# Values by tokens with TensorE transposes, decays by scans and shifted weight bits in a gated linear-memory layer with a dense expert

## The chip, the cores and the metric

The kernel runs on one core of a Trainium2 chip. The metric is the device time of one execution in microseconds, as the median of several runs. Engines are named as in the profile: PE is TensorE, PEld its weight loads, DVE is VectorE, ACT is ScalarE, POOL is GpSimd, SP is SyncE, whose queue issues most of the DMAs.

## The reference

Two layers follow each other, all in float32. The first is a recurrence over 768 positions in 4 batches of 8 heads with 40 dimensions. For every chain (batch and head) and position:

```python
m_new = maximum(f + m, i)
f_stab, i_stab = exp(f + m - m_new), exp(i - m_new)
C = f_stab * C + i_stab * outer(v, k)
n = f_stab * n + i_stab * k
y = sigmoid(o) * (C @ q) / maximum(abs(n @ q), 1)
```

The second takes the 3072 tokens with 320 features (8 heads of 40) through a dense layer:

```python
h = x @ w_in                       # 320 -> 2048
g = maximum(h, 0) + log1p(exp(-abs(h)))
out = g @ w_out                    # 2048 -> 320
```

The weights arrive as 64-bit words and are turned into single precision on the chip.

## The kernel before, in words

**Steps and tiles.** A step is one batch and one chunk of 128 positions; there are 24, in the order of `ORDER`. Three steps form a tile of 384 tokens, so there are 8 tiles. For a step the kernel makes the masked product of queries, keys and decays (the scores), multiplies it with the gated values and the carried state, divides by the normaliser, multiplies with the sigmoid of the output gate, and writes the result, split into a high and a low float32r part, to `X` with features on partitions. For each tile `products` (L922) then runs 16 blocks: 8 products `hp` of 384 columns (L978), two softplus on ScalarE and a difference on VectorE, and 9 products `po` of 320 columns (L949), 3 in float32 for the first tile.

**The first three steps** (tile 0, `first_tile` from L715) stand by themselves. `first_gates` scans the gates of 128 positions for 32 chains. `first_decays` (L441) lays out the logarithms by a GpSimd mask, sums them on TensorE (`fb`, L455), takes the exponential on ScalarE (L459) and masks again on GpSimd (L460). `scores_pairs` (L577) and `weigh` (L573) follow, `values` (L614) gives values with tokens on partitions, and `split_x` (L700) turns them with three TensorE transposes (`xp`, L706).

**The 21 later steps** (`later_step`, L806) take chunks in two halves of 64 positions. `decays` reads the decay factors broadcast from DRAM, `decay` scans them on VectorE. `scores` (L590) makes 16 state products (L600) and 16 score products (L606). `values_late` (L633) makes 16 products `yq` (L642) that have the values' dimensions on partitions and tokens on columns. `values_wide` copies them, writes them to DRAM (L664), `read_wide` reads them back in the layout of `X` with the normaliser repeated on 16 partitions each (L671 to L679), and `finish_wide` and `end_wide` normalise, gate and split on VectorE (L681 to L698). The output gate of these steps comes transposed (`oT`).

**Weights.** Each of 16 blocks of 640 columns is made of a scaled high word (ScalarE, L218 or L220), three low bits (ScalarE L225 or L230, or GpSimd L227, by the table `Q`), a second scaling for the blocks made later (L233), and an OR on VectorE (L236); then high and low parts follow.

**What sets the order.** The program is recorded in order (`in_order`, L113), so each engine runs its instructions as they were issued. The tables `F` (opening), `W`, `M`, `N` (steps of tiles 3 and later, of tile 1, of tile 2), `Q`, `CI` and `CO` give each piece a place, counted in TensorE products; `tick` (L906) issues what is due. Before a tile's first block, everything that its `X` needs is issued, due or not (L967).

PSUM has 8 banks: three for `hp`, two for all else (`pa`), three for `po`.

Of the kernel before, what the change touches and what calls it, by code (L numbers as in the profile page):

```python
# [8 lines left out]
F32 = mybir.dt.float32  # L9
# [24 lines left out]
C = L // 2  # L34
PP = 64
EP = 48
# [8 lines left out]
def mlstm_moe_kernel(  # L45
# [4 lines left out]
    vko: bass.AP,  # L50
    gates: bass.AP,
    oT: bass.AP,
# [25 lines left out]
    eye = nc.gpsimd.affine_select(  # L78
# [4 lines left out]
    nc.gpsimd.memset(near, 0.0)  # L83
    for base in (0, -C):
        nc.gpsimd.affine_select(
            near, near, pattern=[[0, H], [-1, C]], compare_op=ALU.not_equal, fill=1.0, base=base, channel_multiplier=1
        )
# [15 lines left out]
    fg0 = cpool.tile([NCHAIN, L], F32, name="fg0")  # L103
# [26 lines left out]
    def first_gates():  # L130

        fg = fg0
        ig = p1.tile([NCHAIN, L], F32, tag="sig", name="ig0")
        m = p1.tile([NCHAIN, L + 1], F32, tag="y1", name="m0")
        nc.sync.dma_start(fg, gates[0, :, 0:L])
        nc.sync.dma_start(ig, gates[1, :, 0:L])
        nc.vector.memset(m[:, 0:1], -1e30)
        yield
        nc.vector.tensor_tensor_scan(m[:, 1:], fg, ig, m[:, 0:1], ALU.add, ALU.max)
        nc.vector.tensor_tensor(fg, fg, m[:, 0:L], op=ALU.add)  # L140
        nc.vector.tensor_tensor(fg, fg, m[:, 1:], op=ALU.subtract)
        nc.vector.tensor_tensor(ig, ig, m[:, 1:], op=ALU.subtract)
        nc.vector.tensor_copy(m_end, m[:, L : L + 1])
        nc.vector.memset(fg[:, 0:1], 0.0)
        nc.scalar.activation(ig, ig, AF.Exp)
        pg = ps_a.tile([128, 2, NCHAIN], F32, tag="pa", name="pg0")
        nc.tensor.transpose(pg[:, 1], fg, ident[:NCHAIN, :NCHAIN])
        nc.tensor.transpose(pg[:, 0], ig, ident[:NCHAIN, :NCHAIN])
        nc.scalar.copy(lT, pg[:, 1])
        nc.scalar.copy(gT[:, 0, :], pg[:, 0])  # L150
        done.add(("gT", 0))
        yield
        nc.scalar.activation(fg, fg, AF.Exp)
        nc.vector.memset(fg[:, 0:1], 0.0)
        done.add("fg0")
        yield


    def later_gates():
# [11 lines left out]
        nc.vector.tensor_tensor(fg, fg, m[:, 0:w], op=ALU.add)  # L171
        nc.vector.tensor_tensor(fg, fg, m[:, 1:], op=ALU.subtract)
        nc.gpsimd.tensor_tensor(ig, ig, m[:, 1:], op=ALU.subtract)
        yield Q["GR1"]
        need("fg0")
        nc.scalar.copy(fs[:, 0:L], fg0)
# [16 lines left out]
        pg = ps_a.tile([128, NC - 1, NCHAIN], F32, tag="pa", name="pg")  # L193
# [16 lines left out]
    def single(raw, n, dst=None, slope=False):  # L210
# [74 lines left out]
    def lows():  # L285

        yield Q["LB"]
        for u in range(NF // 2):
# [4 lines left out]
    W = dict(FB=-80, LOAD=-67, Y=-29, SCAN=4, VI=11, VW=16, IQ=20, SP=24, SPD=12, CN=31, CD=36, CE=37, CF=42, YQ=53,  # L293
             YQD=-32, EV=15, YD=61, YD1=3, RD=96, RY=11, RZ=1, NM=138, FIN=146, XH=19, XL=18)
    M = dict(FB=-23, LOAD=-50, Y=-9, SCAN=3, VI=-10, VW=10, IQ=25, SP=27, SPD=12, CN=33, CD=43, CE=49, CF=50, YQ=54,
             YQD=3, EV=47, YD=69, YD1=-30, RD=79, RY=-95, RZ=26, NM=116, FIN=128, XH=-9, XL=15)
    N = dict(FB=-26, LOAD=-57, Y=-7, SCAN=9, VI=-16, VW=22, IQ=23, SP=28, SPD=8, CN=30, CD=34, CE=39, CF=60, YQ=55,
             YQD=6, EV=17, YD=67, YD1=-32, RD=84, RY=-22, RZ=10, NM=125, FIN=150, XH=-9, XL=14)
    Q = dict(Gi0=68, Go0=50, Gi1=-42, Go1=1, Gi2=-47, Go2=36, Gi3=38, Go3=7, Gi4=6, Go4=18, Gi5=-8, Go5=31, Gi6=-10,
             Go6=7, Gi7=4, Go7=35, B3=40, B4=84, B5=125, B6=260, B7=300, B8=368, B9=446, B10=528, S0=-375, S1=-292,  # L300
             S2=-195, GT=-381, GL=52, LB=214, LS=33, SPD=-12, OF0=1, OF1=19, GR0=25, GR1=82, GR2=29, GR3=-26, GR4=18,
             GR5=38, LG=10, FS0=-51, FS1=25, FSW=-14, CI=-48, CO=-4, CS=34, K0=-23, K1=-29, CF=15, RC=-17, RS=92,
             B2=-20, B11=620, GT2=92, GL2=108, FS2=-31, GR6=-1, Hi0=-20, Ji0=63, Hi1=34, Ji1=78, Hi2=16, Ji2=34,
             Hi3=-12, Ji3=49, Hi4=-8, Ji4=-16, Hi5=36, Ji5=136, Hi6=-16, Ji6=107, Hi7=-67, Ji7=20)
# [778 lines left out]
```

## Time and profile before

| | us |
|---|---|
| runs (three) | 462.61 median, 462.57 to 463.05 |
| profiled execution, first to last instruction | 460.2 |
| TensorE busy | 433.4 (94%) |
| VectorE busy | 303.9 (66%) |
| ScalarE busy | 211.2 (46%) |
| GpSimd busy | 137.2 (30%) |

The span of the profiled execution, 460.2, is 2.4 below the median of the runs, which also hold what lies around the first and the last instruction. Busy time is an average over very different stages: 40 us ahead of the first tile's products, the first tile, in which the weights are still being prepared, and seven tiles in which TensorE never stops. A view that cuts the span into stages therefore comes first. In a timeline row the first number is the start, the second the length of the merged group, and "x32" counts its records. A float32 product leaves two records, a transpose and a float32r product one.

### The profile page before, as it was taken

The page shows a single profiled execution, that of the slowest core. Times are in us where ns is not written, and L with a number is a line of the kernel's source. Part 1 is how long each engine was busy: PE and PEld are TensorE (multiplying, and loading weights), DVE is VectorE, ACT ScalarE, POOL GpSimd, SP SyncE. Part 2 cuts the span into 40 slices and gives each one's busy share as a digit, 9 for nine tenths or more (in the row PEclk, how much of TensorE's full clock was granted, in tenths as well). Part 3 has the DMA queues.
Part 4 walks back from the last instruction along what each step waited for, and adds up shares of the span by engine and source line. Part 5 has one row for each costly group of instructions (what it writes and reads, how often), then busy time and mean ns, then how long its engine had stood idle before and what let it go on. Part 6 is the DMA issues. An engine that isn't in the chain of part 4 may idle for free.

```text
span 460.2 us, 10555 instructions
## 1 busy us (share of the span) xinstructions
PE 433.4 (94%) x4266; PEld 402.9 (88%) x4266; DVE 303.9 (66%) x577; ACT 211.2 (46%) x416; POOL 137.2 (30%) x152
## 2 busy tenths in 40 slices
PE   5756799899999999999999999999999999999997
PEld 4555587677999999999999999999999999999996
DVE  4657488998987967766776867656876678242121
ACT  2727778784233642355333733463333543333332
POOL 8646078455531131233122312302223111000000
PEclk9975999999999999999999999999999999999999
DMA  7954967587656564654464263555374220101001
GB/s 200 333 188 115 274 197 246 147 214 168 178 180 182 154 151 122 164 144 96 150 185 117 74 204 108 129 143 138 105 196 129 78 78 19 41 0 46 0 1 43
DMA packets 38139, 62.55 MB, mean 136 GB/s; under 512 B 5626, under 2 KB 20258, under 8 KB 38090
## 3 DMA queue, kind: packets, MB, share of 16 engines
q1 hardware_dynamic: 25958, 53.62, 41.3%
q10 hardware_dynamic: 12132, 8.26, 6.3%
q8 instruction: 33, 0.54, 0.5%
q14 instruction: 16, 0.13, 0.1%
HBM read 53.60 MB, written 8.26 MB: 134 GB/s over the span
## 4 chain that ended last, share of the span: by engine, by line
PE 81%; DVE 9%; ACT 3%; POOL 3%; issue 2%; DMA 0%; SPq 0%; POOLq 0%; DVEq 0%; ACTq 0%
PE hp L978 36%; PE po L949 34%; PE yq L642 4%; PE sp L606 2%; PE sp L600 2%; POOL v L564 1%; DVE wof L236 1%; PE yp L619 1%; PE wm L723 1%; DVE wih L271 1%; PE fb L455 1%; DVE wil L269 1%; DVE mv L611 1%; DVE nm L685 1%; DVE gw L494 1%
## 5 line engine op out<-in xcount | busy, mean ns | idle before, releaser
L978 PE MATMUL hp<-X,wih 128*128 128x384 f32 x768 | 181.7, 344 | 4.0 <-ACT X L708 2.8
L978 PEld LDWEIGHTS hp<-X,wih 128*128 128x128 f32 x768 | 133.9, 189 | 9.0 <-ACT X L708 3.2
L854 ACT ACTIVATE gh<-hp 128x384 fp32r<-128x384 f32 x112 | 55.0, 491 | 181.8 <-PE hp L978 175.0
L858 DVE TENSOR_TENSOR gl<-hp,gh 128x384 fp32r<-128x384 f32 x112 | 61.6, 555 | 74.0 <-ACT hp L855 73.1
L949 PE MATMUL po<-wol,gh 128*128 128x320 f32 x336 | 71.2, 311 | 0.0
L949 PE MATMUL po<-woh,gl 128*128 128x320 f32 x336 | 70.3, 309 | 0.0
L949 PE MATMUL po<-woh,gh 128*128 128x320 f32 x336 | 69.8, 308 | 0.0
L978 PE MATMUL hp<-X,wil 128*128 128x384 f32 x256 | 66.6, 339 | 0.1
L500 POOL TENSOR_TENSOR vw<-vt,gw 128x328 f32<-128x328 f32 x23 | 21.7, 944 | 134.3 <-DVE gw L491 123.0
L564 POOL TENSOR_TENSOR v<-v,flast 40x328 f32<-40x328 f32 x37 | 38.2, 1032 | 69.4 <-DVE v L567 53.7
L949 PEld LDWEIGHTS po<-woh,gh 128*128 128x128 f32 x336 | 57.3, 188 | 0.1
L949 PEld LDWEIGHTS po<-woh,gl 128*128 128x128 f32 x336 | 54.9, 188 | 0.2
L949 PEld LDWEIGHTS po<-wol,gh 128*128 128x128 f32 x336 | 54.5, 188 | 0.5
L855 ACT ACTIVATE hp<-hp 128x384 f32<-128x384 f32 x112 | 54.5, 487 | 0.0
L978 PEld LDWEIGHTS hp<-X,wil 128*128 128x128 f32 x256 | 46.4, 189 | 0.9 <-DVE wil L269 0.5
L611 DVE TENSOR_TENSOR mv<-sp,pw 64x256 f32<-64x256 f32 x84 | 31.8, 417 | 14.7 <-PE sp L606 14.2
L482 POOL TENSOR_TENSOR v<-vt,gT 64x328 f32<-64x328 f32 x42 | 33.6, 801 | 22.5 <-DMA vt<-in_vko 19.6
L381 DVE TENSOR_TENSOR mv<-mv,fc 64x512 f32<-64x512 f32 (+1 forms) x42 | 39.1, 930 | 1.1 <-DMA fc<-fc_d 0.5
L949 PE MATMUL po<-wof,gh 128*128 128x320 f32 x96 | 28.5, 440 | 3.9 <-ACT v L544 2.7
L567 DVE TENSOR_TENSOR v<-v,sp 40x164 f32<-40x164 f32 x74 | 23.9, 323 | 12.0 <-POOL v L564 10.7
L439 DVE TENSOR_TENSOR_SCAN pw<-fb,near 128x512 f32<-128x512 f32 x21 | 26.4, 1255 | 3.8 <-DMA fb<-fz_d 3.8
L949 PEld LDWEIGHTS po<-wof,gh 128*128 128x128 f32 x96 | 17.6, 189 | 10.8 <-ACT v L544 3.0
(126 smaller groups left out, 439.9 us busy)
## 6 DMA issues: line engine op xcount, KB each, us to landing
qk<-in_qk SPq DMA_DIRECT2D x21, 416.0 KB
vt<-in_vko SPq DMA_DIRECT2D x23, 324.0 KB
fb<-fz_d SPq DMA_DIRECT2D x42, 128.0 KB
wi<-in_wts SPq DMA_DIRECT2D x8, 640.0 KB
wo<-in_wts SPq DMA_DIRECT2D x8, 640.0 KB
eg<-in_oT SPq DMA_DIRECT2D x7, 576.0 KB
out<-ob SPq DMA_DIRECT2D x24, 160.0 KB
yd<-y ACTq DMA_DIRECT2D x36, 96.0 KB
```

The lines of the kernel that those rows point to most:

```text
L381: nc.vector.tensor_tensor(z.mv[ch][r], z.mv[ch][r], z.fc[r], op=ALU.mult)
L439: nc.vector.tensor_tensor_scan(pw.rearrange(flat), fb.rearrange(flat), eye.rearrange(flat), 0.0, ALU.mult, ALU.add)
L482: nc.gpsimd.tensor_tensor(vi, v1[r], g[r], op=ALU.mult)
L500: nc.gpsimd.tensor_tensor(z.vw, v1, z.gw.broadcast_to([128, H, E]), op=ALU.mult)
L564: nc.gpsimd.tensor_tensor(heads(whole), old, f, op=ALU.mult)
L567: nc.vector.tensor_tensor(dst[i], dst[i], z.cps[ch][dims(i)], op=ALU.add)
L611: nc.vector.tensor_tensor(half(z.mv[ch][r], i), sps[i][r], half(z.pw[r], i), op=ALU.mult)
L854: nc.scalar.activation(gh, hp, AF.Softplus)
L855: nc.scalar.activation(hp, hp, AF.Softplus)
L858: nc.vector.tensor_tensor(gl, hp, gh, op=ALU.subtract)
L949: nc.tensor.matmul(po[j], a[:, j * 128 : (j + 1) * 128], w, start=first, stop=(last and left[j] == 0))
L978: nc.tensor.matmul(hp, a, r, start=(i == 0), stop=(i == len(seq) - 1))
```

## The change

Later steps' values come out with tokens on partitions, as those of the first tile do: weights and moving operand of `yq` change places (L661 of the changed kernel), the output gate is loaded by tokens, normalising and gating happen in `values` on 8-column and 320-column tiles, and `split_x` transposes on TensorE. The way over DRAM goes. The values of a step are issued right ahead of the scores of the next one (`products` in `later_step`). The feature order of `X` changes to a block of 32 dimensions and one of 8 per head, and the rows of `w_in` with it. Two of the three first decay tables are now made by 16 small products that spread the factors (`spread_decays`) and four VectorE scans from PSUM (`scanned_decays`); the third stays with sums (`summed_decays`). The low bits of weights come from a VectorE shift where they came from GpSimd or, in the opening, from ScalarE. The two PSUM pools become one of five banks. The sizes of the tables `F`, `W`, `M`, `N` and `Q` are all new; five instead of seven warm-up products stand at another place.

```diff
-    ps_h = ctx.enter_context(tc.tile_pool(name="ps_h", bufs=3, space=PSUM))
+    ps_h = ctx.enter_context(tc.tile_pool(name="ps_h", bufs=5, space=PSUM))
-    ps_a = ctx.enter_context(tc.tile_pool(name="ps_a", bufs=2, space=PSUM))
...
-        if slope:
-            nc.scalar.activation(sg, top, AF.Copy, scale=1.0 / 32, bias=-31.0 / 64)
-        elif Q["G" + n] % 2:
+        by = 0 if slope else Q["G" + n] % 3
+        if by == 0:
+            nc.vector.tensor_scalar(sg, raw[:, :, 0], 29, None, op0=ALU.logical_shift_right)
+        elif by == 1:
             nc.gpsimd.tensor_scalar(sg.bitcast(F32), top, -15.5, 1.5 * 2.0**28, op0=ALU.add, op1=ALU.add)
...
+    def spread_decays(zs):
...
+        for p in range(HG):
+            for j, (z, i) in enumerate((z, i) for z in zs for i in range(2)):
+                r = slice(j * NCHAIN, (j + 1) * NCHAIN)
+                c = j * NCHAIN + z.b * H + i * HG + p
+                one = ident[r, c : c + 1].broadcast_to([NCHAIN, 128])
+                nc.tensor.matmul(z.fbs[i][:, p, :], one, fe0[r], start=True, stop=True)
+
+    def scanned_decays(z):
+        flat = "p h t -> p (h t)"
+        z.pws = []
+        for i in range(2):
+            pw = p2.tile([128, HG, L], F32, tag="pw", bufs=4, name=f"pw{z.n}_{i}")
+            nc.vector.tensor_tensor_scan(
+                pw.rearrange(flat), z.fbs[i].rearrange(flat), ident4.rearrange(flat), 0.0, ALU.mult, ALU.add
+            )
...
+        yy = ps_h.tile([128, H, E], F32, tag="hp", name=f"yq{z.n}")
+        for h in range(H):
+            for ch in range(2):
+                k = slice(0, 128 if ch else PP + D)
+                nc.tensor.matmul(yy[rows(ch), h, :], z.mv[ch][k, h, :], heads(z.v[ch][k])[:, h, :], start=True, stop=True)
...
-        nc.gpsimd.tensor_tensor(z.sig, z.sig, nq.broadcast_to([128, H, D]), op=ALU.mult)
+        nc.gpsimd.tensor_tensor(sig, sig, nq.broadcast_to([128, H, D]), op=ALU.mult)
         yield
         z.x = work(z, p1, "x", [128, 3 * L], "x", p2, "gl")
-        nc.vector.tensor_tensor(z.x[:, 0:DM].rearrange("p (d h) -> p h d", h=H), yy[:, :, 0:D], z.sig, op=ALU.mult)
-        nc.vector.tensor_copy(z.x[:, DM : 3 * L], z.x[:, 2 * L : DM])
...
+        for lo, hi, two, dst in ((0, DW, 1, z.x[:, 0 : 2 * L]), (DW, D, 2, z.x[:, 2 * L : 3 * L])):
+            w = [128, two, H, hi - lo]
+            nc.vector.tensor_tensor(
+                dst.rearrange("p (two h d) -> p two h d", two=two, h=H),
+                yy[:, :, lo:hi].unsqueeze(1).broadcast_to(w),
+                sig[:, :, lo:hi].unsqueeze(1).broadcast_to(w),
+                op=ALU.mult,
+            )
...
+        def products():
+            if ends:
+                next(ends[0][0])
+            ends.append((values(z), split_x(z), z))
+            return scores(z)
...
-            (at["SP"], lambda: scores(z)),
-            (at["YQ"], y),
-            (at["YD"], lambda: yw),
-            (at["RD"], lambda: read_wide(z)),
-            (at["NM"], lambda: finish_wide(z)),
-            (at["FIN"], lambda: end_wide(z)),
+            (at["UP"], lambda: unpark(z)),
+            (at["SP"], products),
```

**TensorE, the opening.** `fb` are the decay sums or spread factors, `sp` scores, `yp` values, `xp` transposes, `wm` warm-up products, `hp` the first tile's products. Before:

```order
L723 MATMUL wm<-ident_79 128x128 x7
L455 MATMUL fb_0_0_175<-pw_0_0_171,later 128x512
...
L585 MATMUL sp_1_0_207<-qk_0_121 128x128
...
L619 MATMUL yp_0_271<-vi_0_221,pw_0_0_179 128x123 x4
...
L706 MATMUL xp_0_304<-ident_79,x_0_300 128x128 x3
L619 MATMUL yp_0_328<-vi_0_257,pw_0_0_167 128x123 x4
...
L706 MATMUL xp_0_355<-ident_79,x_0_352 128x128 x3
L706 MATMUL xp_0_369<-ident_79,x_0_349 128x128 x3
L978 MATMUL hp_0_407<-X_303,wih 128x384
```

After:

```order
L457 MATMUL fb_0_0_165<-fe_92,ident_76 128x128
...
L619 MATMUL sp_1_0_196<-qk_0_121 128x128
...
L484 MATMUL fb_0_0_208<-pw_0_0_157,later 128x512
...
L654 MATMUL yp_0_245<-vi_0_206,ws_0_0_223 128x123 x4
...
L692 MATMUL xp_0_297<-ident_76,x_0_287 128x128 x3
L654 MATMUL yp_0_304<-vi_0_194,ws_0_0_281 128x123 x4
...
L692 MATMUL xp_0_374<-ident_76,x_0_371 128x128 x3
L708 MATMUL wm<-ident_76 128x128 x5
L973 MATMUL hp_0_408<-X_296,wih 128x384
```

Two of six sums are left, and the warm-up has moved from the front to the place right ahead of the first tile.

**VectorE, the opening after the change.** The later gates' scan is `m<-fs,m,ig` and the decay scans are `pw<-fb,ident` (a scan is printed as SCALAR_TENSOR_TENSOR); `ws` are weighed scores, `sgi` low bits, `x` value products.

```order
L172 SCALAR_TENSOR_TENSOR m<-fs,m,ig 32x640
L175 TENSOR_TENSOR fs<-fs,m 32x640
L176 TENSOR_TENSOR fs<-fs,m 32x640
L464 SCALAR_TENSOR_TENSOR pw_0_0_192<-fb_0_0_167,ident_76 128x512
L464 SCALAR_TENSOR_TENSOR pw_0_0_218<-fb_0_0_165,ident_76 128x512
L464 SCALAR_TENSOR_TENSOR pw_0_1_221<-fb_0_1_166,ident_76 128x512
L608 TENSOR_TENSOR ws_0_0_223<-sp_1_0_196,pw_0_0_218 128x512
L608 TENSOR_TENSOR ws_0_1_229<-sp_1_0_197,pw_0_1_221 128x512
L464 SCALAR_TENSOR_TENSOR pw_0_1_237<-fb_0_1_168,ident_76 128x512
L230 TENSOR_SCALAR sgi_274<-wi_142 128x640
```

Four scans and the first shift now stand on this queue; before, four 4-column products (`gw`, L494) stood there behind the later gates' scan, and the weighings behind them.

**TensorE, a later step.** Here step (b, c) is `..._c_`: before, scores of one step and, 1.5 blocks later, its values alone:

```order
L978 MATMUL hp_12_3115<-X_2111,wil 128x384 x2
L600 MATMUL sp_2_2_3125<-vw_2_3110,vt_2_2867 40x41
...
L606 MATMUL sp_2_2_3125<-qk_2_2928 64x64
...
L978 MATMUL hp_12_3115<-X_2111,wih 128x384
...
L978 MATMUL hp_14_3215<-X_2111,wih 128x384 x2
L642 MATMUL yq_2_3218<-mv_2_2_3020,v_1_112 64x64
L642 MATMUL yq_2_3218<-mv_2_2_3020,v_1_112 48x64
...
L978 MATMUL hp_14_3215<-X_2111,wih 128x384 x3
```

After, the values of step 1 with the scores of step 2, and the transposes of step 1 two blocks later:

```order
L661 MATMUL yq_1_1920<-v_1_102,mv_1_1_1454 64x41
L661 MATMUL yq_1_1920<-v_1_103,mv_1_1_1455 64x41
...
L634 MATMUL sp_1_2_1937<-vw_2_1885,vt_2_1468 40x41
...
L640 MATMUL sp_1_2_1937<-qk_2_1793 64x64
...
L944 MATMUL po_0_1252<-wol_1850,gh_15_1866 128x320
...
L973 MATMUL hp_3_2036<-X_1486,wih 128x384 x5
L692 MATMUL xp_1_2043<-ident_76,x_1_2009 128x128 x3
L973 MATMUL hp_3_2036<-X_1486,wil 128x384 x2
```

The values have joined the next scores, and the transposes stand by themselves inside a block.

## Rows read from the trace of the kernel before

**Rows 1.** Busy time by stages (us, engines, granted clock, DMA).
```profile
40.34:53.85 13.51, 10.58 (x85) 8.79 (x85) 6.33 (x11) 11.57 (x22) 2.21 (x2) 0.80 0.93 267
53.85:105.23 51.38, 48.43 (x469) 37.61 (x469) 45.02 (x76) 39.61 (x69) 30.75 (x24) 1.00 0.70 202
105.23:456.77 351.54, 351.05 (x3580) 338.77 (x3580) 227.66 (x444) 142.63 (x294) 77.14 (x86) 1.00 0.41 113
```

**Rows 2.** Granted clock of the page's 40 slices, tenths.
```profile
PEclk9975999999999999999999999999999999999999
```

**Rows 3.** TensorE's timeline, opening and start of the first tile.
```profile
4.97 0.28 PE L147 MATMUL pg<-ident,fg 32*128 32x32 f32 x1 [4.97 <-DVE m L169]
15.26 2.06 PE L585 MATMUL sp<-qk 40*128 40x128 f32 x32
21.60 5.39 PE L619 MATMUL yp<-vi,pw 128*128 128x123 f32 x32
27.60 0.56 PE L706 MATMUL xp<-ident,x 128*128 128x128 f32 x3 [0.60 <-DVE x L629]
27.99 1.88 PE L619 MATMUL yp<-vi,pw 128*128 128x123 f32 x16
40.34 0.69 PE L978 MATMUL hp<-X,wih 128*128 128x384 f32 x1 [2.80 <-ACT X L708]
48.94 0.51 PE L539 MATMUL cp<-vw,k 128*40 128x41 f32 x16
```

**Rows 4.** The chain that ended last: start, length, what.
```profile
5.44 3.29 PE wm L723 x14
...
14.13 2.50 DVE gw L494 x2
```

**Rows 5.** The DMA-issuing queue of SP, opening.
```profile
3.43 0.43 SPq L165 DMA_DIRECT2D fs<-in_gates  x1
```

**Rows 6.** Groups of instructions by line and form: busy us, mean ns, idle before.
```profile
L706 PE MATMUL xp<-ident,x 128*128 128x128 f32 x9 | 2.3, 388 | 6.6 <-DVE x L629 6.6
L439 DVE TENSOR_TENSOR_SCAN pw<-fb,near 128x512 f32<-128x512 f32 x21 | 26.4, 1255 | 3.8 <-DMA fb<-fz_d 3.8
L170 DVE TENSOR_TENSOR_SCAN m<-fs,m,ig 32x640 f32<-32x640 f32 x1 | 1.8, 1750 | 2.7 <-DMA ig<-in_gates 2.7
L171 DVE TENSOR_TENSOR fs<-fs,m 32x640 f32<-32x640 f32 x1 | 1.1, 1070 | 0.0
L574 DVE TENSOR_TENSOR pw<-sp,pw 128x512 f32<-128x512 f32 x6 | 3.8, 671 | 0.0
L623 DVE TENSOR_SCALAR nq<-yp 128x8 f32<-128x8 f32 x3 | 0.5, 164 | 4.5 <-PE yp L619 3.3 <-POOL og L626 1.2
L626 POOL TENSOR_TENSOR og<-og,nq 128x320 f32<-128x320 f32 x3 | 2.2, 723 | 7.4 <-issue 6.7 <-DVE nq L625 0.7
L629 DVE TENSOR_TENSOR x<-yp,og 128x320 f32<-128x320 f32 x3 | 2.8, 935 | 0.8 <-POOL og L626 0.8
L642 PEld LDWEIGHTS yq<-mv,v 128*64 128x64 f32 x168 | 16.5, 137 | 0.0
L642 PEld LDWEIGHTS yq<-mv,v 128*48 128x48 f32 x168 | 15.0, 123 | 0.0
```

**Rows 7.** TensorE's timeline in tile 3: a step's values, a step's scores.
```profile
219.24 0.60 PE L949 MATMUL po<-woh,gl 128*128 128x320 f32 x3
219.76 1.15 PE L642 MATMUL yq<-mv,v 104*64 104x64 f32 x32
220.84 1.14 PE L978 MATMUL hp<-X,wih 128*128 128x384 f32 x5
223.65 1.03 PE L978 MATMUL hp<-X,wih 128*128 128x384 f32 x5
...
231.34 0.60 PE L949 MATMUL po<-woh,gl 128*128 128x320 f32 x3
232.80 1.14 PE L978 MATMUL hp<-X,wih 128*128 128x384 f32 x5
```

More of the change, by code (lines that the diff above doesn't have):

```diff
@@ L319, in mlstm_moe_kernel @@
     Xs = {}
-    V = [[cpool.tile([128, H * E + EP - E + 1], F32, name=f"v{ch}_{k}") for ch in range(2)] for k in range(2)]
+    V = [[cpool.tile([128, H * E], F32, name=f"v{ch}_{k}") for ch in range(2)] for k in range(2)]
     park = cpool.tile([PP + D, B, H * E], F32, name="park")
@@ L439, in scan, with summed_decays @@
         nc.vector.tensor_tensor_scan(pw.rearrange(flat), fb.rearrange(flat), eye.rearrange(flat), 0.0, ALU.mult, ALU.add)
-    def first_decays(z):
-        need(("gT", 0))
+    def spread_decays(zs):
+        need("fe0")
+        banks = iter(((ps_h, "hp"), (ps_h, "hp"), (ps_h, "hp"), (ps_h, "hp")))
+        for z in zs:
+            z.fbs = []
+            for i in range(2):
+                pool, tag = next(banks)
+                z.fbs.append(pool.tile([128, HG, L], F32, tag=tag, name=f"fb{z.n}_{i}"))
+        for p in range(HG):
[7 more added lines that the diff above has]
+        z.pws = []
+        for i in range(2):
+            pw = p2.tile([128, HG, L], F32, tag="pw", bufs=4, name=f"pw{z.n}_{i}")
+            nc.vector.tensor_tensor_scan(
+                pw.rearrange(flat), z.fbs[i].rearrange(flat), ident4.rearrange(flat), 0.0, ALU.mult, ALU.add
+            )
+            z.pws.append(pw)
+            yield
+    def summed_decays(z):
         z.pws = []
@@ L590, in scores @@
     def scores(z):
-        banks = [ps_a.tile([128, HG * L], F32, tag="pa", name=f"sp{i}_{z.n}") for i in range(2)]
+        banks = [ps_h.tile([128, HG * L], F32, tag="hp", name=f"sp{i}_{z.n}") for i in range(2)]
         z.cps = [b[0 : PP + D, HG * C : HG * (C + E)].rearrange("d (p e) -> d p e", e=E) for b in banks]
@@ L652, in values_wide @@
-    def values_wide(z):
-        yq = values_late(z)
-        yield z.at["YQD"]
-        if z.late:
-            z.y = stage.tile([PP + EP, HG, L], F32, tag="wr", bufs=WB, name=f"y{z.n}")
-        else:
-            z.y = p1.tile([PP + EP, HG, L], F32, tag="yy", name=f"y{z.n}")
-        (nc.scalar.copy if z.at["EV"] % 2 else nc.vector.tensor_copy)(z.y, yq)
-        yield "write"
-        z.yd = dpool.tile([EP * H, L], F32, tag="yd", bufs=2, name=f"yd{z.n}")
-        dst = z.yd.rearrange("(d i p) t -> i d p t", p=HG, i=2)
-        for i in range(2):
-            z.queue.dma_start(dst[i], z.y[i * PP : i * PP + EP])
-            done.add(("yd", z.s, i))
-            yield z.at["YD1"]
@@ L703, in split_x @@
         X, ts = Xs[z.t], slice(z.g * L, (z.g + 1) * L)
-        xp = work(z, ps_a, "pa", [128, 3, L], "xp", ps_h, "hp")
+        xp = ps_h.tile([128, 3, L], F32, tag="hp", name=f"xp{z.n}")
         for j in range(3):
@@ L756, in first_tile @@
         ev = dict(
-            wm=warm, zs=zeros, g0=lambda: next(p0), g1=lambda: next(p0), g2=lambda: run(p0),
+            wm=warm, sd=spread, nd=near_diagonals, zs=zeros, g0=lambda: next(p0), g1=lambda: next(p0), g2=lambda: run(p0),
             o0=lambda: next(o0), o0s=lambda: next(o0), o1=lambda: next(o1), o2=lambda: next(o1), lg0=lambda: next(lg), lg1=lambda: next(lg),
@@ L768, in first_tile @@
             ev[f"tk{k}"] = lambda k=k: tick(-15 * k)
-        for k in range(17):
-            ev[f"wp{k}"] = lambda: next(wparts, None)
+        for a, (u, i) in enumerate(tensors[:AHEAD]):
+            g = (weights_out if i else weights)(u, words)
+            for k in range(4 if i else 5):
+                ev[f"w{a}{'abcde'[k]}"] = lambda g=g: next(g, None)
         for i, z in enumerate(zs):
@@ L812, in fetch @@
             load_values(z)
-            unpark(z)
-        def y():
-            for r in yw:
-                if r == "write":
-                    return
-                yield r
         ev = [
@@ L842, in later_step @@
             ev += [(at["CE"], lambda: next(c1)), (at["CF"], lambda: next(c1, None))]
+        if z.s > START[1]:
+            ev += end_of_step(at)
         yield from in_turn(ev)
+        if z.s == NS - 1:
+            yield from in_turn([(at["YQ"], lambda: next(ends[0][0]))] + end_of_step({k: at[k] + at['YQ'] - at['SP'] if k in ('NQ', 'XM', 'XP', 'XH', 'XL') else w for k, w in at.items()}))
     def activation(t, f, hp, put):
@@ L914, in mlstm_moe_kernel @@
     AHEAD = 3
-    def ahead():
-        for u, i in tensors[:AHEAD]:
-            yield from (weights_out if i else weights)(u, words and "softplus" not in done)
-    wparts = ahead()
     def products():
```

278 lines of the change are left out of this document (128 added, 150 removed).

## The prediction, made before the run

> **What bounds the kernel now.** I read the busy time by stages first. From the first matrix product of the second tile to the last (105.23 to 456.77) TensorE is busy for 351.05 of 351.54 us, while VectorE has 228 and ScalarE 143 of them [rows 1]. There every nanosecond that is put on TensorE's queue lengthens the kernel, every one taken off shortens it, and what VectorE, ScalarE, GpSimd or the DMA engines save is worth nothing. The two rows above it hold the first tile: TensorE idles 2.9 us in each of them, 5.9 us in all, and ScalarE is busy 39.6 of 51.4 us in the second one. [...] Last the chain and TensorE's timeline ahead of the first tile: its first product starts at 40.34 [rows 3], and on the chain a pair of 4-column VectorE operations holds 2.50 us [rows 4]. So there are two accounts: 40 us of latency ahead of the first tile, and TensorE's own work after it.
>
> **The opening.** The change takes two of the three first decay tables from TensorE sums, exponentials and GpSimd masks and gives them to VectorE scans. I follow the new order from the gates to the first product; the sums are estimates.
> - The gates of later chunks are now loaded first: two issues of 0.43 on SP's queue [rows 5], so the first gates come some 0.9 us later, and VectorE, on whose last small operation TensorE waits until 4.97 today [rows 3], gets there at about 5.9. The later gates' scan and its two 640-column operations now follow at once and stand ahead of the decay scans: 1.75 + 2 x 1.1 = 4.0 [rows 6], to 9.9.
> - Three decay scans. VectorE's scan of 128x512 takes 1.255 from SBUF [rows 6]; these read PSUM, which no row shows. Below, 0.67, what another 128x512 pass from PSUM takes; above 1.75, the longest scan. I take the same form's 1.255: 3.8, to 13.7. Two weighings at 0.67: 15.0.
> - TensorE makes the values of the first step: 16 of the 32 records that took 5.39, so 2.7, from the first weighing on, to 17.1; then the scores of the other two steps, 2.06 for 32 records [rows 3], to 19.2. Meanwhile come three small operations (0.5), GpSimd's 0.72, VectorE's product of 0.94 behind two weighings (1.3) [rows 6], and three transposes: about 20.8.
> - The other two steps' values: 32 records, 5.4 [rows 3], to 26.2. Then 1.1 of small operations for both, and VectorE's queue as it is ordered: two tiny products, a weight residual, a value product, a shift, the last value product. With 0.94 for each product, 0.84 for the shift (0.671 scaled from 512 to 640 columns, its upper bound; half is the lower) and 0.7 for the residual that makes 4.7 with the small ones, to 30.9, and 0.4 for the transposes.
> - Five warm-up products now stand on TensorE right there: 10 of the records of which 14 took 3.29 [rows 4], 2.35. The first tile begins at 33.7; I take **34.0 instead of 40.3, a gain of 6.3**.
>
> Bounds: if TensorE were at its upper level throughout, the values would take 1.88 per 16 records [rows 3] and the warm-up half, 3.6 less: 30.4. If VectorE is held up as it is today (2.50 for the pair, [rows 4]) once or twice, it is 39.
>
> **The first tile** takes 105.23 - 40.34 = 64.9 today. Its start at the lower clock falls away: the first hidden product lasts 0.69 [rows 3], and of the ten that stand before the end of the fourth slice (46.0) each takes some 0.18 more than the spacing of 0.173 that five in 1.03, the last 0.34, have later [rows 7]: -1.8. Of the 5.9 us of idle I keep half, since the same 16 weight blocks must be prepared in a shorter time by a ScalarE that is at 77% already: -3.0. The scores of step 6 move in ahead of the second tile: +1.1 (below), and they leave the rest. In the order of the change, step 2's values of the second tile (step 5), the scores of step 6, step 5's transposes and the tile's first product stand on TensorE one behind the other with no product between. There it must wait for normalising (0.5), GpSimd (0.72), the value product (0.94), and behind the transposes (0.4) for ScalarE's cast of the same size as the product (put at 0.5): 3.1, of which the scores cover 0.94: +2.2. With three steps at the price below, 0.5, the tile takes 64.9 - 1.8 - 3.0 + 1.1 + 2.2 + 0.5 = 63.9. The second tile starts at **97.9 instead of 105.2: -7.3**.
>
> **Each later step on TensorE.** Today the values stand alone: the slot after the last output product is 219.68 (219.24 plus three spacings of 0.145, which is 0.60 less the last one's 0.31, halved), the next hidden product starts at 220.84, and its first five last 1.14, not 1.03 [rows 7]. So they cost 1.16 + 0.11 = 1.27. Their 32 records run 0.030 apart, 0.96; the other 0.31 is entering and leaving. The scores likewise: from the slot at 231.78 (231.34 is the group ahead) to 232.80, plus 0.11, 1.13.
> - Joined to the scores, one entry and one exit go. I take 0.24 of the 0.31 off, bounds 0.10 and 0.31.
> - The products swap operands: 64-column weights and 41 moving columns, where it was 64- or 48-column weights and 64 moving. If the moving columns set the pace, the nearest row is 41 moving columns on 40-column weights, 16 records in 0.51, or 0.020 each [rows 3]: 0.68 for all with the last one's length, a gain of 0.28. If the weight load sets it, nothing is gained: a load of 64 columns lasts 14 ns longer than one of 48 (137 against 123, [rows 6]), about 0.9 ns a column, so 58 ns for 64, or 29 ns a record with two halves of the array in turn, which is what it is now. I take no gain, since the loads do not get shorter.
> - Three transposes are new. In the opening, at the faster pace, three of them start at 27.60 and the next product at 27.99: 0.39 [rows 3]. Below 0.33 (they may enter as smoothly as one product follows another), above what the rivals give.
>
> Sum: 0.39 - 0.24 = **+0.15 a step**, and 18 of the 21 steps lie behind the first tile: +2.7, less the 1.1 of the scores that moved ahead, +1.6.
>
> What is removed from the other engines (the copy of the values, the write to DRAM and the three reads, the 128x128 reciprocal, two 128x384 products; most of the low bits from GpSimd and ScalarE) lies beside a full TensorE and counts nothing after 105 us. Its use is only that the first tile's weights are not held up more than I assume. PSUM changes from 3 + 2 banks to 5 shared ones; a score bank is held until the carried state has been added, in which time four others are handed out, so I cost it at nothing. The transposes follow the values by one to two blocks of TensorE work in most tiles (about 5 us), against the 3.1 of their chain; that is the cover, and where it is thin (the first tile) I counted the wait.
>
> **The sum.** 460.2 - 7.3 + 1.6 = 454.5 of span. The median of the runs, 462.61, is 2.4 above the profiled span; with that, **456.9 us**.
>
> **Rivals.**
> - *The values get cheaper.* The moving columns set the pace: 21 x 0.28 = 5.9 less, **451**. For it: 16 records of 41 columns in 0.51; against it: those had 40-column weights. [...]
> - *The opening gains little.* VectorE carries scans, weighings, shifts and residuals one behind the other, and if it is held up as today the first tile starts at 39: 5 us are lost, **462**. For it: the 2.50 us pair [rows 4], four scans on the path; against it: the weighings, values and copies lose their GpSimd partners in part.
> - *The transposes block TensorE, and the kernel gets slower.* Where they stand between full-array products of another kind they may not pipeline; each lasts 388 ns by itself on average [rows 6], so three hold 1.16 instead of 0.39: 21 x 0.77 = 16 more, **473**. It decides from 0.27 a step more than I count (5.7 / 21), a block of 0.66. Against it: 0.39 for three in the one place at the faster pace. [...]
>
> **Chances.** My forecast (452 to 461) 0.58; cheaper values 0.14; a poor opening 0.13; blocking transposes 0.12; the last two together 0.03. A measurement of this kernel tells about 0.2% from no change, 0.9 us, so faster means below 461.7. Faster: 0.58 + 0.14 + 0.06 of the poor opening = 0.78; same: 0.04; slower: 0.03 + 0.12 + 0.03 = 0.18. The range 449 to 463.5 takes in cheaper values with a somewhat better opening, and the poor opening; it leaves out the blocking transposes, the double case and the end of the poor opening, 0.18, and 0.02 below.
>
> **What would show it.** First product of the first tile at 34 (30 to 39), of the second at 98; about 2 us of TensorE idle right ahead of the latter, on the transposes. After it hardly any idle, values and scores as one block of about 2.0 us, transposes of about 0.4. I am wrong if the first tile's time grows past 68 (weights late), if the transposes' block is past 0.66, or if TensorE waits for value products in the later tiles.

## The result and the profile after

The change makes the kernel **slower**, by 1.1%: 467.64 us (median of four runs, 465.75 to 468.43) against 462.83 of the kernel before beside it, a ratio of 1.0106 with a 95% interval of 1.0077 to 1.0135. The profiled execution spans 466.3. I had forecast 456.9 and put 0.78 on faster; the time lies outside the range of 449 to 463.5.

The page of the changed kernel: busy times, and the granted clock by slices (tenths).

```profile
PE 434.1 (93%) x4349; PEld 411.3 (88%) x4349; DVE 267.2 (57%) x582; ACT 199.9 (43%) x391; POOL 136.2 (29%) x166
PEclk9988989997999999999999999999999999999999
```

TensorE is busy as long as before (433.4), VectorE 37 us less, and only slices of the first quarter are marked below 9. The span is 6.1 us longer than before; the stages say where. Busy time by stages of the changed kernel: window, length, then busy us of TensorE, its weight loads, VectorE, ScalarE, GpSimd, the granted clock, DMA share, GB/s. The first row is the first tile, the second what follows up to 461.0, shortly before the last products.

```profile
34.57:109.01 74.44, 60.99 (x630) 49.42 (x628) 52.41 (x103) 51.28 (x90) 32.50 (x36) 0.93 0.69 194
109.01:461.00 351.99, 351.99 (x3559) 344.29 (x3560) 191.03 (x430) 131.21 (x274) 84.92 (x99) 0.99 0.30 82
```

The first tile's first product comes at 34.57 (before 40.34, [rows 3]): 5.8 us are gained. The tile then takes 74.4 us where it took 64.9, and TensorE idles in it for 74.44 - 60.99 = 13.45 us where it idled 5.9 [rows 1]. The second tile starts at 109.01 instead of 105.23. From there on TensorE has hardly a gap, as before. By these figures the opening gains 5.8 us, the first tile loses 9.6, and what follows loses 2.3, of which 1.6 is a start at a granted clock of 0.50 (below). So the loss is made in the first tile and at its end. TensorE's longest waits between 33 and 115 (engine, tile, line, who came last: us, times, longest):

```profile
PE xp L692 <- DVE x L679: 5.5, 3, 3.3
PE hp L973 <- DVE wih L276: 2.8, 2, 1.8
PE pg L199 <- ACT ig L182: 2.6, 1, 2.6
PE hp L973 <- ACT wih L265: 1.1, 1, 1.1
```

**One place: step 3's scaling.** The DMA-issuing queue of SP, then VectorE, then TensorE (start, length, what, in brackets the idle time before and who ended it):

```profile
43.14 0.43 SPq L255 DMA_DIRECT2D wi<-in_wts  x1
43.62 0.43 SPq L255 DMA_DIRECT2D wo<-in_wts  x1
44.09 1.28 SPq L377 DMA_DIRECT2D fc<-fc_d  x2
```

```profile
53.24 1.41 DVE L382 TENSOR_TENSOR mv<-mv,fc 64x512 f32<-64x512 f32 x2 [6.07 <-DMA fc<-fc_d]
56.81 0.81 DVE L241 SCALAR_TENSOR_TENSOR sgi<-magi,sgi 128x640 uint32<-128x640 uint32 x1
60.41 0.60 DVE L276 TENSOR_TENSOR wih<-sgi,wih 64x128 fp32r<-64x128 f32 x2
```

```profile
58.33 0.62 PE L973 MATMUL hp<-X,wih 128*128 128x384 f32 x2 [1.05 <-ACT wih L265]
60.75 0.79 PE L973 MATMUL hp<-X,wih 128*128 128x384 f32 x3 [1.80 <-DVE wih L276]
```

The two small loads of step 3's decays (`fc`) are issued right behind two weight loads of 640 KB each and land 9 us later. VectorE, which works its queue in order, stands still for 6.07 us, and the conversion of the next weights, which needs no `fc`, stands behind. TensorE gets those weights 1.05 and 1.80 us late.

**Another place: the boundary.** TensorE, then VectorE, ahead of the second tile:

```profile
101.75 1.13 PE L661 MATMUL yq<-v,mv 104*64 104x41 f32 x32
107.57 0.87 PE L692 MATMUL xp<-ident,x 128*128 128x128 f32 x3 [3.28 <-DVE x L679]
109.01 1.97 PE L973 MATMUL hp<-X,wih 128*128 128x384 f32 x5 [0.57 <-ACT X L694]
```

```profile
103.33 0.69 DVE L382 TENSOR_TENSOR mv<-mv,fc 40x512 f32<-40x512 f32 x1 [0.70 <-DMA fc<-fc_d]
104.05 0.17 DVE L671 TENSOR_SCALAR nq<-yq 128x8 f32<-128x8 f32 x1
104.57 1.48 DVE L645 TENSOR_TENSOR mv<-sp,pw 64x256 f32<-64x256 f32 x4
106.31 0.66 DVE L597 TENSOR_TENSOR v<-v,sp 40x164 f32<-40x164 f32 x2 [0.26 <-POOL v L594]
107.00 0.62 DVE L679 TENSOR_TENSOR x<-yq,eg 128x256 f32<-128x256 f32 x2
```

Step 5's values are there at about 102.9. Their normalising (L671) stands on VectorE behind step 6's scaling, which waits for its `fc`; their products with the gate (L679) stand behind step 6's weighings and state sums. So TensorE, with no product left to do, waits 3.28 us for the products and 0.57 for the cast. It then starts the second tile at a granted clock of 0.50 (from 107 to 111; before, the tile's first 2.52 us are at 1.00): the fourteenth product comes 4.11 us behind the first (113.12), where it came 2.52 behind it before. That is 1.6 us more.

### The profile page after: what moved, and what is told of

Read it like the earlier page. It is cut to its first block, busy times and chain, and to the rows that moved or that the text cites. A ratio compares the mean times of both kernels' runs of the same rounds, so it can differ in the third digit from the quotient of the medians.

```text
span 466.3 us, 10604 instructions
## 1 busy us (share of the span) xinstructions
PE 434.1 (93%) x4349; PEld 411.3 (88%) x4349; DVE 267.2 (57%) x582; ACT 199.9 (43%) x391; POOL 136.2 (29%) x166
## 4 chain that ended last, share of the span: by engine, by line
PE 78%; DMA 11%; DVE 4%; ACT 4%; SPq 1%; issue 1%; POOL 1%; ACTq 0%; POOLq 0%; DVEq 0%
PE hp L973 35%; PE po L944 32%; PE yq L661 4%; DMA fc<-fc_d 4%; DMA wo<-in_wts 3%; DMA wi<-in_wts 2%; PE sp L640 2%; DMA k<-in_vk 2%; PE sp L634 2%; PE xp L692 2%; DVE mv L645 1%; DVE wil L274 1%; ACT sgi L238 1%; ACT X L694 0%; DVE wof L241 0%
## 5 line engine op out<-in xcount | busy, mean ns | idle before, releaser
L973 PE MATMUL hp<-X,wih 128*128 128x384 f32 x768 | 183.6, 348 | 4.5 <-DVE wih L276 2.8
L973 PEld LDWEIGHTS hp<-X,wih 128*128 128x128 f32 x768 | 137.1, 192 | 7.9 <-DVE wih L276 3.5
L674 POOL TENSOR_TENSOR eg<-eg,nq 128x320 f32<-128x320 f32 x24 | 17.7, 740 | 102.7 <-DVE nq L673 85.7
L382 DVE TENSOR_TENSOR mv<-mv,fc 64x512 f32<-64x512 f32 (+1 forms) x42 | 36.1, 860 | 7.5 <-DMA fc<-fc_d 6.8
L510 POOL TENSOR_TENSOR v<-vt,gT 64x328 f32<-64x328 f32 x42 | 35.9, 855 | 4.1 <-DMA vt<-in_vk 1.4
L594 POOL TENSOR_TENSOR v<-v,flast 40x328 f32<-40x328 f32 x37 | 33.1, 895 | 12.6 <-ACT v L557 5.3
L661 PEld LDWEIGHTS yq<-v,mv 104*64 104x64 f32 (+1 forms) x672 | 21.5, 139 | 5.1 <-issue 5.1
```

The costliest lines, as they stand in the source:

```text
L382: nc.vector.tensor_tensor(z.mv[ch][r], z.mv[ch][r], z.fc[r], op=ALU.mult)
L510: nc.gpsimd.tensor_tensor(vi, v1[r], g[r], op=ALU.mult)
L594: nc.gpsimd.tensor_tensor(heads(whole), old, f, op=ALU.mult)
L661: nc.tensor.matmul(yy[rows(ch), h, :], z.mv[ch][k, h, :], heads(z.v[ch][k])[:, h, :], start=True, stop=True)
L973: nc.tensor.matmul(hp, a, r, start=(i == 0), stop=(i == len(seq) - 1))
```

## The experiments

Two theories. **A**: the first tile lost its time to order: on queues that are worked in order, something that waits stands ahead of something that is due. **B**: 16 weight blocks must be converted in the first tile, and the engines and loads can't do it faster; what is taken from one wait comes back as another.

### Step 3's decays ahead of the weights

```diff
-            (at["Y"], lambda: load_inter(z)),
+            (at["Y"] - 13 * (z.s == START[1]), lambda: load_inter(z)),
```

> One thing changes: on SP's queue the two loads of step 3's last-step decays (fc, 64x512 and 40x512) are issued ahead of the two 640 KB weight loads that stood before them. Theory A (the first tile lost time because queues that are worked in order put something early that waits in front of something that is due): VectorE's wait of 6.07 us on fc until 53.24 falls below 2, the weight residuals behind it come earlier, TensorE's waits for wih of 1.05 and 1.80 at 58 to 61 mostly go, and the second tile starts 2.5 to 4 us earlier: 463.5 to 465. Theory B (16 weight blocks have to be converted in the first tile, and ScalarE and VectorE cannot do it faster, so what is taken from one wait comes back as another): VectorE's wait goes, but the second tile starts within 1 us of 109.0: 467 to 468.

Measured: 463.86 us, ratio 1.0046 (1.0028 to 1.0064). VectorE's wait falls from 6.07 to 1.86, and the residuals come 3.1 us earlier, 0.6 of it because this execution's first tile starts earlier. TensorE's waits for `wih` fall from 3.9 to 1.9:

```profile
47.97 2.31 DVE L382 TENSOR_TENSOR mv<-mv,fc 64x512 f32<-64x512 f32 x2 [1.86 <-DMA fc<-fc_d]
57.32 0.60 DVE L276 TENSOR_TENSOR wih<-sgi,wih 64x128 fp32r<-64x128 f32 x2
```

Between the two ratios lie 0.6%, 2.8 us, and the intervals are apart: A, for the order of four DMA issues.

### Step 5 ends by itself

```diff
-        if z.s > START[1]:
+        if z.s > START[1] and z.s != START[2]:
...
-        if z.s == NS - 1:
+        if z.s in (START[2] - 1, NS - 1):
+            at = dict(at, YQ=60, XP=53, XH=60, XL=69) if z.s < START[2] else at
```

> One thing changes: step 5's values (last step of the second tile) are issued by themselves, among the output products of blocks 8 and 9 of the first tile, and its normalising, value products and transposes follow from there; the scaling, scores and weighings of step 6 stay at their due times, which now fall into the second tile. Theory A: the idle time of TensorE from 102 to 110 (6 us, of which 3.28 waits for step 5's value product behind step 6's scaling and weighings on VectorE) goes, and with it the start at the lower clock (about 1 us); a separate block of values costs 0.2 more: the kernel is 5 to 6.5 us faster, 461 to 463. Theory B: TensorE then waits for weights instead (wih, woh or the activation); 465.5 or more.

Measured: 460.6 us, ratio 0.998 (0.9951 to 1.0009), 1.3% below the change, 5.8 us. TensorE has no gap ahead of the second tile, and the first five products there take 1.27 us (1.97 in the change). That fits the 5.8: the waits of 0.40, 3.28 and 0.57 at the boundary and the 1.6 at the lower clock make 5.85. The output products of the first tile's last two blocks still stand behind the second tile's first two hidden blocks:

```profile
36.03 0.67 PE L974 MATMUL hp<-X,wih 128*128 128x384 f32 x1
88.79 1.13 PE L661 MATMUL yq<-v,mv 104*64 104x41 f32 x32
104.64 1.27 PE L974 MATMUL hp<-X,wih 128*128 128x384 f32 x5
```

In the profiled execution, one of the longest of the ten (463.78), the tile is 68.6 us long (36.03 to 104.64), 5.8 less than in the change, 1.1 of it because step 6's scores now come behind its end.

### Both

> Both of the edits before together. Theory A: the gains add, 7.5 to 10.5 us, 457 to 460, below the kernel before the change; the first tile takes 64 to 67 from its first product to the first of the second tile. Theory B: 465 or more.

Measured: 459.5 us, ratio 0.9947 (0.9931 to 0.9963): faster than the kernel before. The first tile takes 66.6 us; its row, and TensorE's waits of over 0.5 us in it:

```profile
34.95:101.54 66.59, 58.27 (x564) 47.16 (x564) 48.25 (x92) 50.79 (x89) 28.99 (x32) 0.97 0.68 200
```

```profile
PE pg L199 <- ACT ig L182: 2.2, 1, 2.2
PE xp L692 <- DVE x L679: 2.1, 2, 1.3
PE hp L974 <- DVE wih L276: 2.1, 2, 1.1
PE hp L974 <- ACT wih L265: 0.9, 1, 0.9
PE hp L974 <- POOL wih L276: 0.7, 1, 0.7
```

The gains nearly add: 1.6% or 7.4 us together, 8.6 one by one. So A holds for these two places: the same work in another order. There are 8.3 us of idle time left.

### The low bits back to GpSimd

```diff
-        by = 0 if slope else Q["G" + n] % 3
+        by = 0 if slope else 1 if n in ("o1", "i2", "o3", "o5", "o6", "o7") else 2
```

> One part of the change is undone: the low bits of five of the weight tensors behind the first three (o1, o5, i6, o6, o7), which VectorE shifts make in the change, come from GpSimd (four, and o3 too) or ScalarE (i6) as they did before; nothing else differs. Theory A: these shifts stand at places where VectorE has time, so nothing moves by more than 1 us: 466.5 to 468.5. Theory B: if VectorE's load is what holds the weights up, taking 2.5 us of shifts off it makes the first tile 1.5 to 2.5 us shorter (465); if the slower makers hold them up instead, it gets 2 us or more longer (470 or more).

Measured: 469.0 us, ratio 1.0152 (1.0128 to 1.0177), against 1.0106 (1.0077 to 1.0135): 2.1 us slower at the middle, with intervals that touch. At the boundary TensorE now waits 1.72 us for GpSimd's state values (`vw`), where it waited 0.40. They are late through a chain over four engines: a low bit of 2.40 on GpSimd, ScalarE's second scaling behind it (98.92), VectorE's OR, which waits 3.80 for that, and behind the OR on VectorE's queue the small product `gw` that `vw` needs:

```profile
96.49 2.40 POOL L232 TENSOR_SCALAR sgo<-wo 128x640 f32<-128x640 uint8 x1
99.88 1.31 DVE L241 SCALAR_TENSOR_TENSOR wof<-mago,sgo 128x640 uint32<-128x640 uint32 x1 [3.80 <-ACT sgo L238]
103.29 1.02 POOL L530 TENSOR_TENSOR vw<-vt,gw 128x328 f32<-128x328 f32 x1 [2.79 <-DVE gw L519]
104.37 0.52 PE L634 MATMUL sp<-vw,vt 64*40 64x41 f32 x32 [1.72 <-POOL vw L530]
```

Without the shifts the kernel gets no faster, so they are not the cause of the loss; whether they gain something, intervals that touch don't tell. The time lies between the numbers that the two theories gave.

### Two more waits taken away

`pg` later on TensorE, and normalising ahead of the weighings, on top of both:

```diff
+        yield -1000 - 20
         pg = ps_h.tile([128, NC - 1, NCHAIN], F32, tag="hp", name="pg")
...
                 next(ends[0][0])
+                if z.t == 1:
+                    next(ends[0][0])
...
-            (at["NQ"], lambda: next(ends[0][0])),
+            (at["NQ"], lambda: next(ends[0][0], None)),
```

> On top of the two edits together: the five small transposes of the later gates (pg) stand behind the first hidden block on TensorE instead of behind its first product, and the normalising of steps 3 and 4 stands ahead of the next step's weighings on VectorE instead of behind them. Theory A: TensorE's wait of 2.17 us for pg goes, and of its two waits for the value products (1.34 and 0.81) at least 1.5 us: 3 to 4 us, 455.5 to 457. Theory B (what is left of the first tile is set by the weights): the waits for wih grow by nearly as much, 458.5 to 460. In between, a split: the weights come no earlier, so of the 3.7 us about 2 are lost again to wih, 457.5 to 458.5.

Measured: 461.25 us (459.14 to 462.83), ratio 0.9976 (0.9955 to 0.9997). The waits for `pg` and for value products are gone (0.3 left), and nothing is gained: the tile takes 68.0. TensorE's waits in it:

```profile
PE hp L977 <- DVE wih L277: 3.0, 2, 1.9
PE hp L977 <- POOL wih L277: 2.4, 2, 1.7
PE po L948 <- ACT v L575: 1.5, 1, 1.5
PE hp L977 <- ACT park L575: 0.9, 1, 0.9
PE hp L977 <- ACT wih L266: 0.5, 1, 0.5
```

The waits for `wih` grew from 3.7 to 5.9, and two for ScalarE's copies appeared, 2.4 together: what the two edits took away (2.2 and 1.8) came back, about half of it as waits for weights. My expectation for A failed here. B names the right kind of result, but the time lies above the range that I gave for it too, and whether the copies are late because of the weights or of the moved order, no run tells.

### Who holds the weights up

On top of the run before: all low bits by VectorE shifts (`by = 0`), then also the small residuals by VectorE.

```diff
-        by = 0 if slope else Q["G" + n] % 3
+        by = 0
```

> On top of the four edits together: the low bits of the seven weight tensors that ScalarE still makes (0.91 to 0.93 us each) and of one that GpSimd makes come from VectorE shifts too (0.47 each). If ScalarE is what holds the weights of the first tile up (it is busy 14.4 of 17 us from 50 to 67 with one pair of tensors after the other), its 6.4 us less let the weights come earlier, TensorE's waits of 5.9 us for wih fall by half or more: 456.5 to 458.5. If VectorE holds them up (12.9 of the same 17 us), the 3.7 us more on it make them later: 462 or more. If the loads do (the raw buffers and SP's order), nothing changes: 460 to 462.

Measured: 465.34 us (462.44 to 468.52), ratio 1.0098 (1.0058 to 1.0138); the profiled execution is the shortest of the five, with a span of 460.7 (459.6 in the run before), so the trace shows little of the 4 us between the medians. ScalarE's busy time from 50 to 67 falls from 14.4 to 10.4, and the weights come no earlier. On VectorE a shift now waits 5.92 us for its load, and the scaling of step 3, which began at 47.03 in the run before, stands behind it:

```profile
51.49 0.49 DVE L231 TENSOR_SCALAR sgo<-wo 128x640 uint32<-128x640 uint32 x1 [5.92 <-DMA wo<-in_wts]
52.31 1.40 DVE L383 TENSOR_TENSOR mv<-mv,fc 64x512 f32<-64x512 f32 x2
```

It is the pattern of the change's first place once more, with the parts exchanged. Whether VectorE's added 3.7 us alone would have cost anything, the run can't tell.

```diff
-             B11=659, GT2=153, GL2=42, FS2=-39, GR6=-40, Hi0=0, Ji0=1, Hi1=34, Ji1=0, Hi2=1, Ji2=1, Hi3=0, Ji3=0, Hi4=-8,
-             Ji4=0, Hi5=0, Ji5=1, Hi6=0, Ji6=1, Hi7=0, Ji7=1)
+             B11=659, GT2=153, GL2=42, FS2=-39, GR6=-40, Hi0=0, Ji0=1, Hi1=34, Ji1=0, Hi2=1, Ji2=0, Hi3=0, Ji3=0, Hi4=-8,
+             Ji4=0, Hi5=0, Ji5=0, Hi6=0, Ji6=0, Hi7=0, Ji7=0)
```

> As the run before, and the small weight residuals of units 2, 5, 6 and 7 are made by VectorE (0.60 for the pair) instead of GpSimd (1.45 to 1.91 for the pair). If GpSimd's own slowness makes TensorE's two waits for its residuals (1.67 and 0.70), they go: 1.5 to 2 us faster than the run before. If the weights are late before they get to GpSimd, the waits return under VectorE's name: within 0.7 us of the run before.

Measured: 463.77 us (461.5 to 465.4), ratio 1.0047 (1.0027 to 1.0068). The middle is 1.6 us better than the run before, but the profiled span is 1.3 longer, and the intervals overlap: inconclusive. In the traces the waits for `wih` fall from 7.1 to 3.9 us, and those for ScalarE's copies and for value products rise from 3.0 to 5.5: once more a wait that went came back under another name.

### The weight loads one place earlier

```diff
-             fetch=31, fetch2=162, fetch3=225, tk6=126,
+             fetch=31, fetch2=162, fetch3=225, fetch4=235, tk6=126,
...
-            fetch=fetch_next, fetch2=fetch_next, fetch3=fetch_next,
+            fetch=fetch_next, fetch2=fetch_next, fetch3=fetch_next, fetch4=fetch_next,
```

> On top of the four edits together (order on SP, step 5's own end, pg and normalising; low bits as in the change): each weight load from the sixth on is issued one place earlier on SP's queue, the sixth ahead of the write of the decays (fz), which waits on VectorE for 9.5 us while a raw buffer is already free. If the loads hold the weights of the first tile up (the DMA share falls in just that stretch, and ScalarE then waits 3.16 and 1.51 us for loads), TensorE's waits for wih (5.9 us in the run with the four edits) fall to 3.5 or less and the kernel to 457 to 459. If the converting engines hold them up, the weights wait in front of ScalarE and nothing changes: 460 to 462.

> The same on top of the first two edits alone (459.5 us): if the loads hold the weights up, 1.5 to 2.5 us faster, 457 to 458; if the converting engines do, 459 to 460.

Measured: 459.99 us, ratio 0.9968 (0.9951 to 0.9984), on the four edits; **458.16 us, ratio 0.9922 (0.9896 to 0.9947), on the first two**, the lowest median of the study. There the sixth load is issued at 31.55 instead of 44.41. The tile's row:

```profile
34.62:100.06 65.44, 58.08 (x565) 47.26 (x564) 49.13 (x92) 50.93 (x89) 28.59 (x32) 0.96 0.73 197
```

The waits for `wih` fall from 3.7 to 2.4 us, on the four edits from 5.9 to 4.6, each by one trace. That suggests that the loads are part of it. But the steps of the two results (1.2 and 0.4 us by the ratios) are within their intervals and less than I had expected: 458.16 lies between the two ranges that I gave, 459.99 at the edge of "nothing changes". So a gain of the earlier load is not shown. What sets the rest stays open: these runs don't tell the conversion's engines from the raw buffers, and none had a fourth raw buffer.

### The prices on TensorE

Transposes made twice, and value products made twice, the first time with half of the moving columns; each in the 18 steps from the third tile on.

```diff
-        for j in range(3):
+        for j in range(3 * (1 + (z.s >= START[2]))):
+            j %= 3
```

> The changed kernel with the three transposes of each of the 18 steps from the third tile on made twice (the second time over the first). My price: one of them more costs its spacing of about 0.083 us (a block of three cost 0.25 + 0.08), so 18 x 0.25 = 4.5 us more, 472. If transposes block TensorE for their own length of 0.388: 18 x 1.16 = 21 more, 488.

```diff
+                if z.s >= START[2]:
+                    nc.tensor.matmul(yy[rows(ch), h, 0:21], z.mv[ch][k, h, :], heads(z.v[ch][k])[:, h, 0:21], start=True, stop=True)
```

> The changed kernel with every value product of the 18 steps from the third tile on made twice, the first time with 21 of the 41 moving columns (overwritten by the second). If the load of 64 weight columns sets the pace, the short one costs as much as the long one, 0.030 us: 18 x 32 x 0.030 = 17 us more, 485. If the moving columns do, it costs half of the 0.020 that 41 columns took in the opening at most: 18 x 32 x 0.010 = 6 us more, 474.

Measured: 473.81 us, ratio 1.0262 (1.0231 to 1.0292), for the transposes, and 485.84 us, ratio 1.0522 (1.0494 to 1.0551), for the products. Six transposes and the product behind them; then the start of the doubled values and of the scores behind them:

```profile
142.89 0.82 PE L693 MATMUL xp<-ident,x 128*128 128x128 f32 x6
143.47 1.11 PE L974 MATMUL hp<-X,wih 128*128 128x384 f32 x5
```

```profile
195.26 0.30 PE L662 MATMUL yq<-v,mv 104*64 104x21 f32 x4
195.40 0.30 PE L663 MATMUL yq<-v,mv 104*64 104x41 f32 x4
...
197.28 0.52 PE L634 MATMUL sp<-vw,vt 64*40 64x41 f32 x32
```

Six transposes hold 0.58, three hold 0.24 (below): 0.34 more a step, 6.1 in 18; the profiled span grew by 4.7 and the ratio by 1.6%, 7.2 us. With two runs only that is 4.7 to 7.2, somewhat more than my 4.5 and far from the 21 of blocking ones. The 64 records of values hold 2.02 us instead of 1.07 for 32: one with 21 columns costs what one with 41 does, 0.030. That is 18 x 0.95 = 17.1; the profiled span grew by 18.8 (485.1 against 466.3), the ratio by 4.2%, 19 us. So the moving columns don't set the pace. A fixed time per record doesn't either: with the same 41 moving columns on 40-column weights, records run 0.020 apart [rows 3]. What differs is the number of weight columns, and with it the recorded length of a load: a median of 138 ns for these 64-column ones, 117 for the 40-column ones (L661; `cp` of [rows 3]). That the weight load sets the pace is my reading of that; no run varied the weights alone.

## Why the prediction was wrong, by its own steps

**The opening: right.** First product at 34.57; I took 34.0. The terms missed singly and made up for each other, so that the 0.6 by which it is off is partly luck: three scans from PSUM hold 3.43, or 1.14 each (I took 1.255), the values run at the faster pace from 17.5 on (1.88 per 16 records, the lower bound, at a granted clock of 1.00), and VectorE delays the last two steps' products more than I counted (TensorE waits 3.16 for them).

**The later steps: right.** Rows of the second and the third tile's products in the changed kernel (the same blocks hold as much in the fourth tile), a step's transposes and a step's values with the next one's scores:

```profile
143.23 0.61 PE L944 MATMUL po<-woh,gl 128*128 128x320 f32 x3
143.68 0.49 PE L692 MATMUL xp<-ident,x 128*128 128x128 f32 x3
143.92 1.11 PE L973 MATMUL hp<-X,wih 128*128 128x384 f32 x5
...
189.30 0.60 PE L944 MATMUL po<-woh,gl 128*128 128x320 f32 x3
189.82 1.13 PE L661 MATMUL yq<-v,mv 104*64 104x41 f32 x32
191.82 1.13 PE L973 MATMUL hp<-X,wih 128*128 128x384 f32 x5
```

Reckoned as in the prediction, from the slot behind the last output product: the joined block holds 191.82 - 189.74 = 2.08, with the 0.10 by which the next five products are late 2.18; values and scores apart held 1.27 + 1.13 = 2.40, so -0.22 (I took -0.24). The transposes hold 0.25, with 0.08 for the next five 0.33 (I took 0.39). Net +0.11; I took +0.15. The time from the second tile's first product to the end of the span agrees to within some 0.6: 460.2 - 105.23 = 355.0 before, 466.3 - 109.01 = 357.3 in the change, +2.3, of which 1.6 is the start at the lower clock; I took +1.6 without it. In the fastest version, where step 6's scores stand behind the boundary again and the second tile's first five products take 1.27 us, it is 457.7 - 100.06 = 357.6: 2.6 more, where I took 18 x 0.15 = 2.7 and the rows above give 18 x 0.11 = 2.0.

Two rivals fall with these rows. The values did not get cheaper: 0.030 us a record with 41 moving columns as with 64, and with 21. The 0.020 that 41 columns take on 40-column weights [rows 3], which spoke for that rival, does not hold on these weights.

Transposes don't block: three cost 0.33, and the granted clock is 0.99 for the stage, 1.00 from 115 on. On the clock the runs show only that three transposes between dense products don't lower it, not what transposes by themselves would do.

**The first tile: wrong, and with it the result.** The step that failed is "64.9 - 1.8 - 3.0 + 1.1 + 2.2 + 0.5 = 63.9": measured 74.4, which is 10.5 of the 11.8 us by which the span missed the forecast of 454.5.
- *"Of the 5.9 us of idle I keep half"*, and the boundary's *"+2.2"*: together I allowed 5.2 us of idle time, and there were 13.45. The new tables of numbers had other queue orders, and I followed the order of VectorE's and SP's queues only as far as the first product and never through the tile. The `fc` loads behind two weight loads, and normalising behind another step's scaling and weighings, both stood in that order, and [rows 1] already said that VectorE and ScalarE had little to spare there. Moving `fc` alone gave 2.8 us back, ending step 5 by itself 5.8, both 7.4. The 459.5 us with both are still 2.6 above the forecast, and what holds those stays open.
- *"Its start at the lower clock falls away"*, the -1.8, came only in part. The start at 34.57 was at a granted clock of 1.00 (34.5 to 37; before, 0.50 from 40 to 44), but after one product TensorE waited 2.56 us for `pg`, which needs the later gates from ScalarE, and then ran at a granted clock of 0.57 and 0.50 until 41. The prediction has no term for `pg`.
- *The boundary's wait* was priced by its own chain of 3.1 less cover. The chain's own operations were priced about right, but on VectorE it is not alone: step 6's scaling, its weighings of 1.48 and state sums of 0.66 stand in it. Waits of 0.40, 3.28 and 0.57 came of it.
- *TensorE's own time* in the tile is 61.0, I had 63.9 - 5.2 = 58.7. The idle time costs twice here: behind the three long gaps (2.56; 1.05 and 1.80; 3.28 and 0.57) the granted clock is at about 0.5 for some 3 to 5 us (0.50 from 37.8 to 41, from 62 to 65 and from 107 to 112), behind gaps of 1.0 to 1.2 it stays at 1.00 (70 to 76). Over the tile it is 0.93; in the fastest version it is 0.96, with 58.1 us of TensorE's time, which hold step 6's scores (1.1) no more.
- *An earlier start isn't kept.* I let the tile begin 6 us earlier and lose some idle time too. But the engines that convert the weights had as much to do in the tile as before (ScalarE 51.3 us against 51.2, VectorE 52.4 against 51.4): where the prediction has "most of the low bits from GpSimd and ScalarE" removed, seven of sixteen blocks still have them from ScalarE and one from GpSimd. And the weight loads came no earlier: the sixth to ninth loads are issued at 43.14, 43.62, 48.18 and 55.87, where it was 39.94, 45.96, 47.41 and 56.98, the sixth behind the decays' way over DRAM although its buffer was free 12 us before (in the fastest version it is issued at 31.55). When two waits were removed that didn't concern weights, TensorE waited for weights instead (3.7 to 5.9 us). What this bullet is worth in time, no run separates from the others.

I had named "weights late" as what would make me wrong, past 68 us for the first tile, without a chance of its own among the rivals. A rival "the tile ends when its weights are there" at 105 or later would have been on the other side: 105.23 + 355 + 1.6 + 2.4 = 464.

## What to carry to other kernels

A change that moves the tables of an order is to be read on every in-order queue through the whole stage that bounds it, DMA issues included: look for an instruction that waits for a late transfer and ask who stands behind it. A gain in front of a stage may be lost in it if the stage's other inputs are not early too; put a ready time on each of them before adding the gain up. And if a change with good prices comes out slower, look for its order first: here a moved line and a step that ends by itself turned 1.1% slower into 0.5% faster (with one earlier load it was 0.8%, a step within the intervals).

## What was not expected

- Small loads behind large ones landed later than I had thought: two `fc` loads (128 and 80 KB), issued 0.5 us behind two weight loads, were there 9 us later; ahead of them they were there some 6 us after their issue (42.34 to 47.97), and VectorE waited 1.86.
- The opening isn't equally long in each execution: with the same order up to there, the first tile's first product came at 33.93 (`fc` ahead) to 36.03 (step 5's own end) in the profiled ones, and some of the versions differ by more from run to run (458.42 to 463.88 for step 5's own end) than the kernel before the change does (461.03 to 463.41 beside it).
